# Sketch attention and a cosine router: queries sketched like keys, token rows scattered to expert regions, ten expert blocks placed among the attention's ticks

## The chip, the cores and the metric

The kernel runs on one core of a Trainium2 chip. The metric is the device time of one execution in microseconds (us); less is better. The engines are PE (TensorE: matmul; PEld is its weight load), DVE (VectorE), ACT (ScalarE), POOL (GpSimd) and SP (SyncE, which issues DMAs). Each works through its own queue in order.

## The reference

Polynomial sketch attention is followed by a router that sends each token to one of eight experts. All data is f32.

```python
# q, k, v: (4, 4, 1088, 32); S1, S2: (8, 32); expert_emb: (8, 128); w1: (8, 128, 1024); w2: (8, 1024, 128)
def phi(x):
    a = einsum('rd,bhsd->bhsr', S1, x); b = einsum('rd,bhsd->bhsr', S2, x)
    return einsum('bhsi,bhsj->bhsij', a, b).reshape(..., 64)
q_p, k_p = phi(q), phi(k)
kv = einsum('bhsf,bhsd->bhfd', k_p, v);  z = sum(k_p, axis=2)
attn = einsum('bhsf,bhfd->bhsd', q_p, kv) / (einsum('bhsf,bhf->bhs', q_p, z)[..., None] + 1e-6)
x = attn.transpose(0, 2, 1, 3).reshape(4352, 128)
xn = x / (norm(x) + 1e-6);  en = expert_emb / (norm(expert_emb) + 1e-6)
logits = xn @ en.T / tau
idx = argmax(logits, 1);  probs = softmax(logits)
out[idx == e] = probs[:, e] * (relu(x[idx == e] @ w1[e]) @ w2[e])    # for each expert e
```

## The kernel before

The four batches are taken as two pairs (`NM = 2`, index m). A token of a pair is one of 128 partitions in one of 17 chunks (`NC`), so a pair has 17 chunks of 128 tokens and the whole 34 (`NT`). Chunks are worked on in groups of three or four (`K_GROUPS`, `Q_GROUPS`; the last key group has one).

**Loads.** SP issues all loads in order: keys and values of pair 0, its queries, the same for pair 1, then the weights of the eight experts. Keys and queries land one head at a time in `k_sb` and `q_sb`, where the four heads of a chunk lie side by side.

**Keys** (`k_steps`): `tr` turns each chunk with a transpose, `ab` makes both sketches of a chunk in one product with `Sblk` (L270), ACT copies the second sketch to `b_sb`, DVE multiplies the two into the 64 features per head, `kp` (L276), and `kv` sums `kp` times v and a column of ones into PSUM (L288). `kz` is the masked sum of a pair.

**Queries** (`q_steps`): `tr` turns a chunk; `fa` and `fb` (L328) make the features already transposed and as wide as they are after the outer product, with `Sa` and `Sb`, up to 512 tokens at once; their product is `qp` (L340); `nd` multiplies it with `kz` on column halves of the array (L348) and divides, which gives the token rows `x`; `xt` turns those, ACT sums their squares (`ssq`, L367), and `logit` gives eight logits per token (L372).

**Routing.** `pick(m)` finds the expert of each token of a pair as a one-hot `oh`; `gate_tokens(m)` divides by the norm (a square root as a power of one half on POOL, L399), takes the softmax value, multiplies it into the token rows on POOL (L408) and stores them to `x_dram` through SP (L410). After both pairs, `route_and_run_experts` counts and ranks all tokens per expert (L418 to L449), builds the list of tokens of each of 41 blocks (`NBLK`) of 128 slots by one-hot products (L462 to L490), and has `src_i` (rows to fetch), `dst_i` (rows to write) and `exp_i` (the expert of a block). An expert's tokens fill whole blocks; unused slots write nowhere.

**Expert blocks.** Block i: `fetch` gathers 128 rows of `x_dram` with an indirect DMA from POOL (L497), four blocks ahead (`AHEAD`); `turn` transposes them (L503); `weights` copies the expert's weights within SBUF on DVE (L512, L513); `up` has eight products and a Relu on ACT (L522, L523); `down` has eight products (L529), a copy to `y` (L531) and an indirect DMA that scatters the rows to `out` (L532). On PE the order is up(i), turn(i+1), down(i-1).

**Order.** In attention, `put` enters each step in a table of ticks, but a scheduler may move instructions; only from `route_and_run_experts` on are DVE and PE kept in the order written. ACT and POOL are ordered by the scheduler throughout.

Of the kernel before, what the change touches and what calls it, by code (L numbers as in the profile page):

```python
# [21 lines left out]
R = 8  # L22
# [11 lines left out]
K_GROUPS = ((0, 4), (4, 8), (8, 12), (12, 16), (16, 17))  # L34
Q_GROUPS = ((0, 4), (4, 8), (8, 11), (11, 14), (14, 17))
# [3 lines left out]
NOWHERE = 8192.0  # L39
DIGIT = 128  # L40
# [9 lines left out]
def kernel(  # L50
# [28 lines left out]
    def ps_acc(i):  # L79
        return psum.tile([P, 512], F32, tag=f"acc{i}", bufs=1, name=f"ps_acc{i}")  # L80
# [6 lines left out]
    def rows_tile(name):  # L87
        return rows_p.tile([P, NC, H, D], F32, tag="rows", name=name)

    def load_q(m):  # L90

        for i in range(2):
            for h in range(H):
                nc.sync.dma_start(
                    q_sb[m][i * HALF:(i + 1) * HALF, :, h],
                    bass.AP(tensor=q.tensor, offset=q.offset + ((2 * m + i) * H + h) * S * D,
                            ap=[[NC * D, HALF], [D, NC], [1, D]]))


    v_sb = [consts.tile([P, 6, NC, D], F32, name=f"v{m}") for m in range(NM)]  # L100

    def load_k(m, i):
        for h in range(H):
            nc.sync.dma_start(
                k_sb[m][:, i * NK:(i + 1) * NK, h],
                bass.AP(tensor=k.tensor, offset=k.offset + ((2 * m + i) * H + h) * S * D,
                        ap=[[NK * D, P], [D, NK], [1, D]]))

    def load_v(m, i):
        for p in range(2):  # L110
            nc.sync.dma_start(
                v_sb[m][:, 3 * p:3 * p + 2, i * NK:(i + 1) * NK],
                bass.AP(tensor=v.tensor, offset=v.offset + ((2 * m + i) * H + 2 * p) * S * D,
                        ap=[[NK * D, P], [S * D, 2], [1, NK * D]]))

    def load_rest(m):
        for i in range(2):
            r = slice(i * HALF, (i + 1) * HALF)
            at = (2 * m + i) * H * S * D + SK * D
            nc.sync.dma_start(k_sb[m][r, NC - 1],  # L120
                              bass.AP(tensor=k.tensor, offset=k.offset + at, ap=[[D, HALF], [S * D, H], [1, D]]))
            for p in range(2):
                nc.sync.dma_start(v_sb[m][r, 3 * p:3 * p + 2, NC - 1],
                                  bass.AP(tensor=v.tensor, offset=v.offset + at + 2 * p * S * D,
                                          ap=[[D, HALF], [S * D, 2], [1, D]]))
# [4 lines left out]
    for m in range(NM):  # L130
        k_sb[m] = rows_tile(f"k{m}")
        for i in range(2):
            load_k(m, i)
            load_v(m, i)
        load_rest(m)
        q_sb[m] = rows_tile(f"q{m}")
        load_q(m)
        if m == 0:
            nc.sync.dma_start(emb_sb[:], emb)
            nc.sync.dma_start(tau_sb[:], bass.AP(tensor=tau.tensor, offset=tau.offset, ap=[[0, E], [1, 1]]))  # L140
# [9 lines left out]
    for m in range(NM):  # L150
        for p in range(2):
            nc.gpsimd.memset(v_sb[m][:, 3 * p + 2], 1.0)

    mask4 = consts.tile([P, H], F32, name="mask4")
    maskh = consts.tile([P, 2], F32, name="maskh")
    for t in (mask4, maskh):
        nc.vector.memset(t, 0.0)
    for h in range(H):
        nc.vector.memset(mask4[h * D:(h + 1) * D, h:h + 1], 1.0)
    for h in range(2):  # L160
        nc.vector.memset(maskh[HALF * h:HALF * (h + 1), h:h + 1], 1.0)
# [28 lines left out]
    nc.vector.tensor_copy(ST, ps[:, :2 * R])  # L190

    Sblk = consts.tile([P, 6, 2 * R], F32, name="Sblk")
    nc.vector.memset(Sblk, 0.0)
    nc.vector.tensor_mul(Sblk[:, :H], bview(ST, [[0, H], [1, 2 * R]]), bview(mask4, [[1, H], [0, 2 * R]]))
    Sa = consts.tile([P, H, R, R], F32, name="Sa")
    Sb = consts.tile([P, H, R, R], F32, name="Sb")
    for h in range(H):
        nc.vector.tensor_scalar_mul(Sa[:, h], bview(ST, [[1, R], [0, R]]), mask4[:, h:h + 1])
        nc.vector.tensor_scalar_mul(Sb[:, h], bview(ST[:, R:], [[0, R], [1, R]]), mask4[:, h:h + 1])

    half_c = consts.tile([P, NC], F32, name="half_c")
    nc.gpsimd.memset(half_c, 0.5)
    x_dram = tc.dram_tile([N, DM], F32, name="x_dram")

    def iota(shape, pattern, base, mult, name):
# [6 lines left out]
    lane = iota([P, P], [[1, P]], 0, 0, "lane")  # L212
    part = iota([P, 1], [[1, 1]], 0, 1, "part")
    first = iota([P, E], [[-1, E]], E, 0, "first")
    start = iota([P, NT], [[P, NT]], 0, 0, "start")
    lane_b = consts.tile([P, P], BF16, name="lane_b")
    nc.vector.tensor_copy(lane_b, lane)
    tok_i = consts.tile([P, 3, NT], I32, name="tok_i")
    nc.gpsimd.iota(tok_i[:, 0].rearrange("p (m c) -> p m c", m=NM), pattern=[[2 * S, NM], [1, NC]], base=1,
                   channel_multiplier=NC)  # L220
    nc.vector.tensor_scalar(tok_i[:, 1], tok_i[:, 0], 7, None, op0=ALU.logical_shift_right)
    nc.vector.tensor_scalar(tok_i[:, 2], tok_i[:, 0], DIGIT - 1, None, op0=ALU.bitwise_and)
    tok_d = consts.tile([P, 2, NT], F32, name="tok_d")
    nc.vector.tensor_copy(tok_d, tok_i[:, 1:])
    digits = [tok_d[:, d] for d in range(2)]
    before = consts.tile([P, P], F32, name="before")
    nc.vector.tensor_scalar(before, lane, part[:, 0:1], None, op0=ALU.is_gt)
    ones = consts.tile([P, P], F32, name="ones")
    nc.vector.memset(ones, 1.0)
    follows = consts.tile([P, E, NT], F32, name="follows")  # L230
    nc.vector.memset(follows, 1.0)
    nc.vector.memset(follows[:, :, 0:1], 0.0)

    enT = consts.tile([P, 96], F32, name="enT")
    nc.vector.memset(enT, 0.0)

    def prep_emb():
# [4 lines left out]
        nc.gpsimd.tensor_tensor(out=ss, in0=ss, in1=half_c[:E, 0:1], op=ALU.pow)  # L242
# [7 lines left out]
        nc.vector.tensor_copy(enT[:, :E], ps[:, :E])  # L250


    kz = {}
    acc = {}

    def k_steps(m, c0, c1):
# [3 lines left out]
        def tr():  # L260
            ps = ps_small()
            for j in range(n):
                nc.tensor.transpose(ps[:, j * P:(j + 1) * P], k_sb[m][:, c0 + j].rearrange("p h d -> p (h d)"), ident)
            s["kT"] = work.tile([P, 512], F32, tag="xT", name="kT")
            nc.scalar.copy(s["kT"][:, :n * P], ps[:, :n * P])

        def ab():
            ps = ps_small().rearrange("p (j g r) -> p j g r", j=4, r=2 * R)
            for j in range(n):
                nc.tensor.matmul(ps[:, j, :6], s["kT"][:, j * P:(j + 1) * P], Sblk, start=True, stop=True)  # L270
            b_sb = work.tile([P, 4, H, R], F32, tag="b", name="b_sb")
            nc.scalar.copy(b_sb[:, :n], ps[:, :n, :H, R:])  # L272
            s["kp"] = work.tile([P, 4, H, R, R], F32, tag="kp", name="kp")
            for j in range(n):
                a, b = ps[:, j, :H, :R], b_sb[:, j]
                nc.vector.tensor_mul(s["kp"][:, j],  # L276
                                     bview(a, [list(a.ap[1]), list(a.ap[2]), [0, R]]),
                                     bview(b, [list(b.ap[1]), [0, R], list(b.ap[2])]))

        def kv():  # L280
            if c0 == 0:
                acc[m] = [ps_acc(i)[:, :6 * D].rearrange("p (a n) -> p a n", a=2) for i in range(2)]
            for c in range(c0, c1):
                rest = c == NC - 1
                for i in range(2) if rest else (c // NK,):
                    r = slice(i * HALF, (i + 1) * HALF) if rest else slice(0, P)
                    for p in range(2):
                        nc.tensor.matmul(  # L288
                            acc[m][i][:, p],
                            s["kp"][r, c - c0, 2 * p:2 * p + 2].rearrange("s h i j -> s (h i j)"),  # L290
                            v_sb[m][r, 3 * p:3 * p + 3, c],
                            start=c == i * NK and p == 0, stop=rest, skip_group_check=True)
            if c1 == NC:
                for i in range(2):

                    z = consts.tile([P, 2, 2, D + 1], F32, name=f"kz{2 * m + i}")
                    t = acc[m][i]
                    nc.vector.tensor_mul(z[:, :, :, :D], t[:, :, :2 * D].rearrange("p a (h d) -> p a h d", h=2),
                                         bview(maskh, [[0, 2], [1, 2], [0, D]]))
                    zs = t[:, :, 2 * D:2 * D + 1]  # L300
                    nc.vector.tensor_mul(z[:, :, :, D], bview(zs, [list(zs.ap[1]), [0, 2]]),
                                         bview(maskh, [[0, 2], [1, 2]]))
                    kz[2 * m + i] = z.rearrange("p a h d -> p a (h d)")
        return [tr, ab, kv]

    x_sb = {}
# [266 lines left out]
    for i in sorted(at):  # L573
        for f in at[i]:
            f()
# [33 lines left out]
```

## Time and profile before

| | |
|---|---|
| median of 3 runs (lowest, highest) | 307.86 us (307.71, 309.45) |
| profiled execution | 309.62 us, span 307.8 us, granted TensorE clock 0.916 |
| busy in the span | PE 254.5, PEld 230.3, DVE 140.1, POOL 107.2, ACT 86.5 us |
| L522 and L529 (expert products) | 656 records each, 83.6 and 79.8 us |
| L497, L532 (indirect DMAs on POOL) | 41 each, mean 1.17 and 1.01 us |
| L523, L531 (ACT in a block) | mean 1.03 and 0.27 us |
| L512, L513 (weight copies on DVE) | 41 each, mean 0.69 us |
| L340 (qp, 1024 wide), L276 (kp, 256 wide) on DVE | mean 1.21 and 0.42 us |
| loads | 17.8 MB read from HBM; queue q1 24.2% of 16 engines' time |

A row of a group has its line, engine and operation, the tiles by name (out<-in), the shape and count, then busy time, mean duration of one in ns, and the engine's idle time just ahead of them with what ended it. A row of the timeline has its start, its duration, and in brackets the idle time ahead. A window has its length, the busy time and count of each engine, the granted clock, and the share and rate of the DMA engines. A product in f32 shows as two matmul records, a transpose as one. Durations of records on PE overlap.

### The profile page before, as it was taken

What the parts mean: (1) busy time and instruction counts of PE and PEld (TensorE: products, weight loads), DVE (VectorE), ACT (ScalarE), POOL (GpSimd) and SP (SyncE); (2) the same over time, 40 slices, a digit from 0 to 9 for tenths busy, and PEclk for the clock granted to TensorE, in tenths of its full rate; (3) what the DMA queues carried; (4) which work ended last, traced back from release to release, by engine and by line L of the source; (5) the groups of instructions that cost most, each with busy time, mean ns of one, the idle gap of its engine ahead of it and who ended that gap; (6) DMA issues with size and microseconds to landing.
All of it is one profiled execution on the core that took longest, in us unless ns stands there. A gap on an engine that the chain in (4) does not pass through costs nothing. (4 is left out here: it accounts for less than half of the span.)

```text
span 307.8 us, 5515 instructions
## 1 busy us (share of the span) xinstructions
PE 254.5 (83%) x2127; PEld 230.3 (75%) x2127; DVE 140.1 (46%) x345; ACT 86.5 (28%) x195; POOL 107.2 (35%) x103
## 2 busy tenths in 40 slices
PE   0987999999799750125999999999999999999960
PEld 0886777776467530114999999999999999999960
DVE  7334254345464448982344444444444444444400
ACT  1121242332245210001133333333333333333320
POOL 4000000000413034017455666555666556632230
PEclk9999799999999955555799999999999999999995
DMA  6999799993003001102111111111111111210000
GB/s 122 167 136 171 146 135 327 336 345 85 0 2 145 1 2 66 79 0 48 30 34 38 34 37 28 36 30 44 37 30 37 34 40 32 36 25 19 15 2 0
DMA packets 51194, 22.59 MB, mean 73 GB/s; under 512 B 38425, under 2 KB 48676, under 8 KB 50912
## 3 DMA queue, kind: packets, MB, share of 16 engines
q1 hardware_dynamic: 48544, 17.31, 24.2%
q0 software_dynamic: 2624, 4.92, 6.2%
q8 instruction: 17, 0.28, 0.4%
q14 instruction: 9, 0.07, 0.1%
HBM read 17.77 MB, written 4.92 MB: 74 GB/s over the span
## 5 line engine op out<-in xcount | busy, mean ns | idle before, releaser
L522 PE MATMUL ps_big<-xTb,w1b 128*128 128x128 f32 x656 | 83.6, 283 | 1.7 <-issue 1.3
L522 PEld LDWEIGHTS ps_big<-xTb,w1b 128*128 128x128 f32 x656 | 79.8, 199 | 2.4 <-issue 1.7
L529 PE MATMUL ps_acc<-w2b,hT 128*128 128x128 f32 x656 | 79.8, 275 | 0.0
L529 PEld LDWEIGHTS ps_acc<-w2b,hT 128*128 128x128 f32 x656 | 76.4, 192 | 0.0
L523 ACT ACTIVATE hT<-ps_big 128x1024 f32<-128x1024 f32 x41 | 42.1, 1027 | 94.6 <-PE ps_big L522 83.6
L497 POOL DMA_INDIRECT xs<-x_dram,src_i x41 | 48.0, 1170 | 39.4 <-PE ps_t L503 21.4
L532 POOL DMA_INDIRECT out_dram<-y,dst_i x41 | 41.4, 1010 | 50.3 <-ACT y L531 48.4
L505 DVE COPY xTb<-ps_t 128x128 f32<-128x128 f32 x41 | 12.0, 292 | 75.0 <-PE ps_t L503 75.0
L512 DVE COPY w1b<-w_sb 128x1024 f32 x41 | 28.5, 694 | 13.5 <-DVE xTb L505 12.1
L399 POOL TENSOR_TENSOR nrm<-ssq,half_c 128x17 f32<-128x17 f32 x2 | 6.2, 3087 | 65.7 <-ACT sq L367 65.7
L513 DVE COPY w2b<-w_sb 128x1024 f32 x41 | 28.5, 694 | 0.0
L340 DVE TENSOR_TENSOR qp<-a_sb,ps_big 128x768 f32<-128x768 f32 (+1 forms) x10 | 10.6, 1055 | 23.4 <-PE ps_big L328 20.3
L531 ACT COPY y<-ps_acc 128x128 f32<-128x128 f32 x41 | 11.0, 267 | 33.9 <-PE ps_acc L529 33.9
L288 PE MATMUL ps_acc<-v,kp 128*128 128x96 f32 (+1 forms) x144 | 19.8, 295 | 0.8 <-DVE kp L276 0.8
L288 PEld LDWEIGHTS ps_acc<-v,kp 128*128 128x128 f32 (+1 forms) x144 | 18.2, 206 | 2.9 <-DVE kp L276 1.6
L276 DVE TENSOR_TENSOR kp<-ps_t,b_sb 128x256 f32<-128x256 f32 x34 | 12.1, 418 | 14.5 <-ACT b_sb L272 14.5
L469 PE MATMUL ps_acc<-col,row 128*128 128x82 bf16 x34 | 3.0, 269 | 18.3 <-DVE row L466 18.3
L328 PE MATMUL ps_big<-qT,Sa 128*128 128x384 f32 (+1 forms) x40 | 17.3, 556 | 0.0
L367 ACT ACTIVATE sq<-x 128x128 f32<-128x128 f32 x34 | 10.3, 308 | 24.2 <-DVE x L356 24.2
L469 PEld LDWEIGHTS <-row 128*128 128x128 bf16 x34 | 2.3, 138 | 19.7 <-DVE row L466 19.7
L328 PE MATMUL ps_big<-qT,Sb 128*128 128x384 f32 (+1 forms) x40 | 16.5, 534 | 0.0
L503 PE MATMUL ps_t<-ident,xs 128*128 128x128 f32 x41 | 11.5, 281 | 4.2 <-DMA xs<-x_dram,src_i 4.2
(137 smaller groups left out, 220.3 us busy)
## 6 DMA issues: line engine op xcount, KB each, us to landing
w_sb<-in_moe_w_dram SPq DMA_DIRECT2D x16, 512.0 KB, 8.3
q<-in_q_dram SPq DMA_DIRECT2D x16, 136.0 KB, 4.2
x_dram<-x SPq DMA_DIRECT2D x2, 1088.0 KB
k<-in_k_dram SPq DMA_DIRECT2D x16, 128.0 KB, 3.8
v<-in_v_dram SPq DMA_DIRECT2D x8, 256.0 KB, 3.3
xs<-x_dram,src_i POOLq DMA_INDIRECT x41
out_dram<-y,dst_i POOLq DMA_INDIRECT x41
k<-in_k_dram SPq DMA_DIRECT2D x4, 32.0 KB, 3.4
```

What stands on the lines that cost most here:

```text
L276: nc.vector.tensor_mul(s["kp"][:, j], bview(a, [list(a.ap[1]), list(a.ap[2]), [0, R]]), bview(b, [list(b.ap[1]), [0, R], list(b.ap[2])]))
L288: nc.tensor.matmul(acc[m][i][:, p], s["kp"][r, c - c0, 2 * p:2 * p + 2].rearrange("s h i j -> s (h i j)"), v_sb[m][r, 3 * p:3 * p + 3, c], ...
L328: nc.tensor.matmul(ps[:, p, :w], S_[:, 2 * p:2 * p + 2].rearrange("p h i j -> p (h i j)"), s["qT"][:, :w], start=True, stop=True)
L497: nc.gpsimd.indirect_dma_start(out=xs[i][:], out_offset=None, in_=x_dram[:, :], in_offset=bass.IndirectOffsetOnAxis(ap=src_i[:, i:i + 1], ...
L503: nc.tensor.transpose(ps[:, :P], xs.pop(i), ident)
L505: nc.vector.tensor_copy(xT[i], ps[:, :P])
L512: nc.vector.tensor_copy(w1b[i], w1_sb[:, bass.ds(e, 1)].rearrange("p o f -> p (o f)"))
L513: nc.vector.tensor_copy(w2b[i], w2_sb[:, bass.ds(e, 1)].rearrange("p o f d -> p (o f) d"))
L522: nc.tensor.matmul(ps[:, u, j * P:(j + 1) * P], w[:, f * P:(f + 1) * P], x, start=True, stop=True)
L523: nc.scalar.activation(hT[i], ps, ACT.Relu)
L529: nc.tensor.matmul(ps, h[:, f * P:(f + 1) * P], w[:, f], start=f == 0, stop=f == NF - 1)
L532: nc.gpsimd.indirect_dma_start(out=out[:, :], out_offset=bass.IndirectOffsetOnAxis(ap=dst_i[:, i:i + 1], axis=0), in_=y[:], in_offset=None ...
```

## The change

- **Loads and keys.** `k_sb`, `q_sb` hold each head's chunks side by side, so one transpose turns four chunks of one head, and one DMA loads a batch's keys. The seventeenth chunk has tiles of its own (`k_rest`, `q_rest`). v has one column of ones per pair.
- **Queries like keys.** `Sa` and `Sb` are gone. Queries go through the same `turned`, `sketch`, `second`, `features` as keys; a new step `tr_qp` transposes the features, two per chunk.
- **Column halves.** `sketch`, `kv` and `logit` have 64-column stationary operands whose outputs lie in one or the other half of the PSUM partitions.
- **Rows in regions.** The token rows with their eight logits, the sum of squares and the token's number are 138 words in `xg`. `router` picks experts for eight chunks at a time, ranks them with running counts, and `place` scatters each chunk (one indirect DMA on POOL per 128 rows) into the region of its expert in `rows`. `table_early` and `table_late` compute only which region rows a block has.
- **Early blocks.** Ten blocks (`EARLY`) need only full blocks of pair 0's tokens; `table_early` names them, and the others come from `table_late`.
- **Gate at y.** A block computes norm, Exp and sum for its own rows (`norm` with a power on POOL, `up`, `share`), and the gate is the scale of the copy to `y`. The output row's number is the last word of the fetched row.
- **Order.** All of attention, routing and blocks are entered in one table, and PE, DVE, ACT and POOL are kept in that order.

```diff
-K_GROUPS = ((0, 4), (4, 8), (8, 12), (12, 16), (16, 17))
-Q_GROUPS = ((0, 4), (4, 8), (8, 11), (11, 14), (14, 17))
+GROUPS = ((0, 4), (4, 8), (8, 12), (12, 16), (16, 17))
+SPAN = 8
+ROW = DM + E + 2
+EARLY = (NM * NC * P // 2 - E * (P - 1) + P - 1) // P
+LATE = NBLK - EARLY
...
+    def sketch(ps, t, n):
+        for u in range(2):
+            r = slice(u * HALF, (u + 1) * HALF)
...
+                for h in range(H):
+                    nc.tensor.matmul(ps[r].rearrange("p (g h r) -> p g h r", h=H, r=2 * R)[:, :, h],
+                                     t[:, h * P + u * HALF:h * P + (u + 1) * HALF], Sblk, start=True, stop=True)
...
+    def features(ab, b, n, tag):
+        t = work.tile([P, 4, H, R * R], F32, tag=tag, name=tag)
+        nc.vector.tensor_mul(t[:, :n].rearrange("p j h (i k) -> p (j h) i k", i=R),
+                             ab[:, :, 0].unsqueeze(3).broadcast_to([P, n * H, R, R]),
+                             b[:, :n * H].unsqueeze(2).broadcast_to([P, n * H, R, R]))
...
+    def keys(m, c0, c1, put, late):
...
+        put(0, 60, tr)
+        put(1, 51, ab)
+        put(1, 61, b)
+        put(1, 63, prod)
+        put(5 if late else 3, 30, kv)
...
+    def queries(m, c0, c1, put):
...
         def tr():
+            if at == 0:
+                xg[g] = work.tile([P, SPAN, ROW], F32, tag="xg", bufs=3, name="xg")
+            s["qT"] = turned(None if n == 1 else q_sb[m][:, :, c0:c0 + 4], q_rest[m], n, "qT")
+            nc.gpsimd.iota(xg[g].bitcast(I32)[:, own, ROW - 1], pattern=[[1, n]], base=2 * S * m + c0,
+                           channel_multiplier=NC)
...
+        put(0, 61, tr)
+        put(1, 50, ab)
+        put(1, 60, b)
+        put(1, 62, prod)
+        put(3, 10, tr_qp)
+        put(4, 20, nd)
+        put(5, 20, xt)
+        put(5, 80, squares)
+        put(6, 10, logit)
+        put(6, 70, best)
+        if c1 == NC or c1 % SPAN == 0:
+            pick, place = router(m, c1 - at - n, c1)
+            put(6, 71, pick)
+            put(7, 40, place)
...
+        def place():
...
             for j in range(n):
+                d = nc.gpsimd.indirect_dma_start(
+                    out=rows[:, :], out_offset=bass.IndirectOffsetOnAxis(ap=slot[:, j:j + 1], axis=0),
+                    in_=xg[m, c0 // SPAN].bitcast(I32)[:, j], in_offset=None)
+                tc.add_to_no_dep_group("rows", d.ins)
+                if m > 0:
+                    tc.add_to_no_dep_group("early", d.ins)
...
+    def norm(i):
+        rn[i] = work.tile([P, 1], F32, tag="rn", bufs=3, name="rn")
+        nc.gpsimd.tensor_tensor(out=rn[i], in0=xs[i][:, DM + E:DM + E + 1], in1=half_c, op=ALU.pow)
+        nc.vector.tensor_scalar_add(rn[i], rn[i], NORM_EPS)
+        nc.vector.reciprocal(rn[i], rn[i])
...
+    def up(i):
...
         nc.scalar.activation(hT[i], ps, ACT.Relu)
+        p = work.tile([P, E], F32, tag="probs", name="probs")
+        gate[i] = work.tile([P, 1], F32, tag="gate", bufs=3, name="gate")
+        nc.scalar.activation(p, xs[i][:, DM:DM + E], ACT.Exp, scale=rn.pop(i)[:, 0:1], accum_out=gate[i])
...
+    def share(i):
+        nc.vector.tensor_scalar_add(gate[i], gate[i], PROB_EPS)
+        nc.vector.reciprocal(gate[i], gate[i])
...
+    def first_block():
         for i in range(AHEAD):
             fetch(i)
+        norm(0)
         weights(0)
         turn(0)
...
+    def block(i):
+        if i + AHEAD < NBLK:
+            fetch(i + AHEAD)
+        if i < NBLK:
+            up(i)
+        if i + 1 < NBLK:
+            turn(i + 1)
+            weights(i + 1)
+        if i < NBLK:
+            share(i)
+        if i + 1 < NBLK:
+            norm(i + 1)
+        if i > 0:
+            down(i - 1)
...
     tick = 0
+    for g in GROUPS:
+        keys(0, *g, put_at(tick), True)
         tick += 2
+    put_at(tick)(0, 0, prep_emb)
+    for g in GROUPS:
+        keys(1, *g, put_at(tick), False)
+        queries(0, *g, put_at(tick))
         tick += 2
+    put_at(tick)(5, 90, table_early)
+    put_at(tick)(8, 90, first_block)
+    for g in GROUPS:
+        queries(1, *g, put_at(tick))
+        tick += 2
+    put_at(tick)(5, 50, table_late)
+    for i in range(NBLK + 1):
+        put_at(tick)(i - 1, 55, lambda i=i: block(i))
```

The first number of `put` is the tick after the group's own, the second the rank within the tick. So keys of pair 0 start at ticks 0 to 8, keys of pair 1 and queries of pair 0 at 10 to 18, queries of pair 1 at 20 to 28; scatters stand in ticks 19, 23, 25 (pair 0) and 29, 33, 35 (pair 1), eight, eight and one; block i stands in tick 29 + i. The sketches of a tick's keys and queries share one PSUM bank, "ab".

## The prediction

> **What bounds the kernel now.** I read the page's slices first, then busy time by stretches, then the groups by shape, and last the timeline around the routing and at the start of the expert blocks.
>
> ```profile
> PE   0987999999799750125999999999999999999960
> PEclk9999799999999955555799999999999999999995
> 100.00:110.00 10.00, 7.60 (x77) 5.62 (x75) 3.87 (x11) 3.53 (x15) 0.80 (x1) 0.96 0.00 1
> 110.00:120.00 10.00, 2.28 (x5) 1.18 (x4) 7.51 (x20) 0.32 (x1) 4.90 (x2) 0.50 0.01 2
> 120.00:130.00 10.00, 0.79 (x9) 0.61 (x9) 9.52 (x20) 0.00 (x0) 1.21 (x1) 0.50 0.27 111
> 130.00:140.00 10.00, 2.25 (x25) 1.69 (x25) 7.92 (x18) 0.00 (x0) 2.31 (x2) 0.50 0.02 7
> 160.00:170.00 10.00, 10.00 (x92) 10.00 (x91) 3.95 (x8) 3.62 (x5) 6.20 (x6) 1.00 0.13 36
> ```
>
> The columns of a stretch are its length, the busy time of PE, PEld, DVE, ACT and POOL with instruction counts, the granted clock, the DMA share and GB/s. The span has four stages: attention to 110.2 us (PE nearly full), routing to 141.4 (a chain on DVE; PE idle, clock 0.50), 41 expert blocks to 297.6 (PE full; a block starts every 3.68 us: its second halves start at 150.26, 153.94, 157.63), and 10.2 us from PE's last product to the end.
>
> ```profile
> L270 PE MATMUL ps_t<-Sblk,kT 128*128 128x96 f32 x68 | 13.1, 335 | 1.4 <-ACT kT L265 1.4
> L399 POOL TENSOR_TENSOR nrm<-ssq,half_c 128x17 f32<-128x17 f32 x2 | 6.2, 3087 | 65.7 <-ACT sq L367 65.7
> L340 DVE TENSOR_TENSOR qp<-a_sb,ps_big 128x1024 f32<-128x1024 f32 x4 | 4.8, 1206 | 9.5 <-PE ps_big L328 9.5
> L242 POOL TENSOR_TENSOR emb_ss<-emb_ss,half_c 8x1 f32<-8x1 f32 x1 | 0.6, 575 | 18.3 <-ACT emb_sq L241 18.3
> ```
> ```profile
> 75.88 1.98 PE L328 MATMUL ps_big<-qT,Sa 128*128 128x512 f32 x4
> 88.37 1.03 PE L372 MATMUL ps_t<-enT,xT 128*128 128x96 f32 x8
> 89.59 1.21 PE L348 MATMUL ps_big<-kz,qp 128*64 128x66 f32 x32 [0.19 <-DVE qp L340]
> 117.37 3.84 POOL L408 TENSOR_TENSOR x<-x,gate 128x2176 f32<-128x2176 f32 x1 [5.10 <-DVE gate L407]
> 118.04 3.20 DVE L434 TENSOR_TENSOR_SCAN upto<-ones,nb 128x8 f32<-128x8 f32 x1
> 143.15 0.95 POOL L497 DMA_INDIRECT xs<-x_dram,src_i  x1 [0.30 <-issue]
> 144.40 0.95 POOL L497 DMA_INDIRECT xs<-x_dram,src_i  x1 [0.30 <-issue]
> 152.90 1.02 POOL L532 DMA_INDIRECT out_dram<-y,dst_i  x1 [1.02 <-ACT y L531]
> 154.49 1.19 POOL L497 DMA_INDIRECT xs<-x_dram,src_i  x1 [0.57 <-PE ps_t L503]
> ```
>
> Mean durations overlap, so I take pitches from runs of one group: (1.21-0.22)/31 = 0.03 us for a product on a column half, (1.03-0.28)/7 = 0.11 for a full 128-column one, (1.98-0.64)/3 = 0.43 to 0.45 for 512 wide. Each f32 product is two records, a transpose one. POOL issues an indirect DMA every 1.25 us (0.95 + 0.30).
>
> **PE.** Per four chunks the keys cost 28 x 0.11 = 3.1 us before; now 4 transposes, 16 records in ab and 32 in kv on halves: 0.44 + 48 x 0.03 = 1.9. Queries: 16 x 0.11 + 32 x 0.03 + 8 x 0.43 = 6.2 before; now Sa and Sb go, 8 transposes of qp come, ab and logit go to halves: 16 x 0.11 + 64 x 0.03 = 3.7. Over 8.5 groups that is 9.3 against 5.6, 31 us less PE work. If eight neighbours on one half don't overlap (ab only), 16 x 0.03 more, 8 us in all, mostly off the path. Logits at 0.03 is the nearest row; at 0.06, 4 us.
>
> The Trainium skill (TensorEngine Tiling (Array Packing), Key Properties) says that changing the tiling mode drains the array, which speaks against mixing halves and full products. Here the step from the last L348 record to the next full product was 0.15 us (83.913 to 84.063) against 0.03 inside the group; two switches per pair of ticks make 2 us over attention, and I keep them out of the sum, since PE doesn't set the pace there.
>
> **Routing.** L382 to L490, 31.2 us of idle PE, goes; so do the two x_dram stores on SP and both 3.8 us multiplies on POOL. In their place: per eight chunks a pick (some 1.3 us of DVE) and a place (0.7 us), two tables on DVE (13 ops, 3 us; 22 ops, 5.6 us, by rows of 0.17 to 0.48), and 34 scatters on POOL at 1.25 = 42 us. Ten blocks need only batches 0 and 1. SP issues 12 loads per pair of batches instead of 26, in longer pieces; by the 330 GB/s of 50 to 70 us the data of each stage lands ahead of it (at 150 GB/s, the early rate, the last keys land near 40, still in time).
>
> **When the first scatter starts.** Keys begin at 5.9. The one "ab" bank is held from ab through prod, so a group costs 0.5 + 0.25 + kb 0.27 + 0.1 + 1.2 (L340) = 2.4; five with a cold start end near 18.5. prep_emb stands ahead of tick 10's transposes: ACT, POOL, DVE in turn, 2.3 more. A pair of ticks with keys and queries cycles through ab 0.5, 0.25, qb 0.27, both products 2.4, nd on DVE 1.1, xt 0.43, kv 1.0, with hand-overs 6.15 us; PE needs 5.6, ACT 5.5, DVE 5. Pairs of 2.9, 5.0, 6.15, 6.15 bring tick 18 to 41, and nd, best, pick and place of tick 19 take 6.3: 47.3. Bounds: 38 by PE work alone, 58 at the old 9.3 per pair.
>
> **POOL's queue to the first block.** It is now in order by hand. Eight scatters, 10.0; the iota of tick 20 rewrites the same buffer (three xg, six used), so it waits for them to land, 1.5 + 0.5 (L497 from 137.39 landed at 140.5, 1.6 after its end); eight more, 10.0; the iota of tick 24, 2.2; the one scatter of tick 25, 1.25; the iota of tick 28, 2.0; four fetches, 5.0; pow and hand-over, 0.9. That is 33.4. DVE's norm(0) stands ahead of weights(0) and turn(0), 0.35 + 0.3 + 1.4 + 0.3: the first up starts at 83. PE and ACT alone would be there at 72 (Q1 pairs of 5 us, by ACT's 4.64: 2.0 of it squares). Bounds: a scatter at 1.0 or 1.5 gives 78 or 88.
>
> **First up to the eighth, tick 29 to 36.** Their PE work is 7 x 3.68 + 4 of queries = 30 us. But tick 29's eight scatters stand ahead of fetch(4) and pow(1): DVE waits in norm(1) until +13, behind it nd, behind that PE's xt. From there POOL goes fetch, pow, scatter per block; tick 33 puts eight more scatters ahead of pow(5) (near +38), norm(6) near +41, then pick and place; table_late's 5.6 us end near +49, and weights(7) lets up(7) go at +51. Bounds 30 (all hidden) and 65 (scatters at 1.5, pow at its high end of a few per block).
>
> **The other 34 blocks.** PE 3.68 each. POOL per block: fetch 1.2, pow, scatter 1.02, gaps of 0.30. L242 (one element in 8 lanes) gives pow 0.58, L399 (17 in 128) 3.09; two rows make 0.42 + 0.16 per element, so 0.58 is nearest: 3.4 us, hidden by 0.28. pow may also meet DVE's weight copies, as L434 met L408 above (3.2 us for eight numbers): up to 0.7 more, 0.4 per block uncovered, 14 us. ACT (1.03 + 0.5 + 0.27) and DVE (0.29 + 1.4 + 0.6) stay under 3.68. So 34 x 3.68 + 1.95 = 127. The last scatter loses its wait for the one before (297.97 to 299.29): the tail goes from 10.2 to 9.1. After idle spells the clock was 0.50 (110 to 150 us); 1 us for that, 0 to 5.
>
> **Sum.** 83 + 51 + 127 + 9 + 1 = 271 us of span, against 307.8. The profiled execution took 309.6, 1.8 more than its span, and the median of the runs is 1.8 below it, so the forecast of the median is 271.
>
> The rows show an indirect DMA of 1.19 us beside the weight copies (154.49) and of 0.95 without (143.15): 0.25, already in the sum. The Trainium skill (SBUF — State Buffer, Summary: rules for kernel authors) holds that GpSimd's descriptor writing starves while DVE runs a fast copy, which speaks against the change. With the 3.1 us that SBUF — State Buffer (A bandwidth-pool intuition that's wrong) gives for such an overlap, an estimate for the 34 scatters would pass 330 us. I go by the rows.
>
> **Rivals.** *POOL hides:* scatters and waits for xg stay behind other work. For it: POOL is idle until tick 19. Against: the iota and norm chains above. Then 72 + 30 + 127 + 9 = 238.
>
> *Half-way:* pow meets the copies and the last 34 blocks take up to 4.1: 271 + 14 = 285, and up to 300 with scatters at 1.5 (+5 and +7).
>
> *Slower:* POOL sets the pace of every block. Place: fetch, pow, scatter in one queue. At pow 3.09, 5.9 per block: 83 + 3 + 51 + 17 + 34 x 5.9 + 11 = 366. It loses to before from pow = 1.65 on (34 x 0.8 + 8 x 1.07 = 36); or from 0.37 more per indirect DMA (52 x 0.37 early, 34 x 0.52 late), which rows of 552 instead of 512 bytes could bring. For it: L399; against: L242, and 1.0 on every L532.
>
> *The change doesn't do what it says:* early fetches wait for the late scatters. They stand ahead of them in POOL's queue, so they can't.
>
> **How the numbers follow.** Forecast (262 to 282) 0.50; hidden 0.17; half-way 0.20; slower 0.13. 243 leaves about 0.1 of "hidden" below, 300 about 0.1 above. Faster by over 1% 0.85, within 1% 0.02, slower 0.13; the runs before spread by 0.6%, so about 1% can be told.
>
> **What would show it.** Right: POOL's scatters in rows of eight 1.25 apart, the first near 47; DVE waiting on POOL's pow for 10 us twice; PE with a hole near 75 to 83 and thin slices to 134; blocks 3.68 apart after that. Wrong: blocks wider than 3.7 (POOL per block), up(0) before 75 (hidden), or scatters above 1.5.

## The result, and the profile after

The changed kernel takes 333.51 us (median of 4 runs, 332.59 to 334.52) against 307.88 us before: ratio 1.0825, 95% interval 1.0777 to 1.0873. It is slower by 8%; the forecast was 271 us, faster. The profiled execution has a span of 330.7 us.

The slices of the changed kernel (page, part 2) come first: PE, POOL and the granted clock.

```profile
PE   2967887803910391049650099999999999999992
POOL 4010001332332523373433638888888888888632
PEclk9999999965585678558795569999999999999998
```

Before, PE had one hole of 31 us. Now it has four: slices of 8.3 us with 0 or 1 between 65 and 190 us, with the granted clock at 0.5 or 0.6 of full speed somewhere in each. From 196 us on PE is full, as before. Four stretches by engine (columns as in the stretches before):

```profile
70.00:80.00 10.00, 0.00 (x0) 0.00 (x0) 0.73 (x2) 0.00 (x0) 3.11 (x6) 0.50 0.06 21
100.00:110.00 10.00, 0.00 (x0) 0.00 (x0) 2.18 (x8) 0.00 (x0) 4.21 (x7) 0.50 0.08 24
130.00:140.00 10.00, 0.00 (x0) 0.00 (x0) 0.00 (x0) 0.00 (x0) 3.36 (x4) 0.53 0.06 21
250.00:300.00 50.00, 49.99 (x449) 49.83 (x448) 28.71 (x93) 23.05 (x55) 42.64 (x42) 1.00 0.14 36
```

In the holes POOL works about a third of the time (3.1 to 4.2 of 10 us), DVE less (0 to 2.2), the others not at all: this is a chain of waits, not a lack of engine time. POOL's timeline shows what it does in the holes, and the fetches after it:

```profile
55.09 1.07 POOL L475 DMA_INDIRECT rows_dram<-xg,slot  x1 [33.15 <-ACT sq L402]
58.27 0.97 POOL L475 DMA_INDIRECT rows_dram<-xg,slot  x1 [2.11 <-ACT xT L397]
61.33 0.96 POOL L475 DMA_INDIRECT rows_dram<-xg,slot  x1 [2.09 <-DMA rows_dram<-xg,slot]
64.38 0.96 POOL L475 DMA_INDIRECT rows_dram<-xg,slot  x1 [2.10 <-ACT lg L413]
...
109.13 0.96 POOL L563 DMA_INDIRECT xs<-rows_dram,src  x1 [0.30 <-issue]
110.40 0.95 POOL L563 DMA_INDIRECT xs<-rows_dram,src  x1 [0.30 <-issue]
```

A scatter (L475) takes the same 0.96 us of POOL as a fetch (L563), but 2.1 us of idle time stand ahead of it instead of 0.30. The pitch is 3.06 us (about 2.6 in the last row of eight), where the forecast had 1.25. The second and fourth row name ACT as the releaser; ACT had long been done with that span's rows, and the 2.1 us are the same whoever is named. It is the landing of the scatter before. The waits (in all, times, longest) and the groups carry the bill:

```profile
DVE rn L587 <- POOL rn L586: 56.0, 33, 21.9
POOL rows_dram L475 <- DMA rows_dram<-xg,slot: 43.0, 22, 2.2
DVE xg L389 <- DMA rows_dram<-xg,slot: 25.4, 2, 13.8
```
```profile
L586 POOL TENSOR_TENSOR rn<-xs,half_c 128x1 f32<-128x1 f32 x41 | 33.4, 815 | 0.9
...
L475 POOL DMA_INDIRECT rows_dram<-xg,slot x34 | 33.3, 980 | 98.6 <-DMA rows_dram<-xg,slot 43.0 <-ACT sq L402 33.1 <-DVE slot L473 6.9
```

DVE stands up to 21.9 us in `norm`, because the power stands in POOL's queue behind a row of eight scatters. Here are the last of them, a fetch and the power on POOL, then DVE:

```profile
139.52 0.96 POOL L475 DMA_INDIRECT rows_dram<-xg,slot  x1 [2.14 <-DMA rows_dram<-xg,slot]
142.29 0.98 POOL L563 DMA_INDIRECT xs<-rows_dram,src  x1 [1.80 <-DMA rows_dram<-xg,slot]
143.29 0.57 POOL L586 TENSOR_TENSOR rn<-xs,half_c 128x1 f32<-128x1 f32 x1
143.90 0.15 DVE L587 TENSOR_SCALAR rn<-rn 128x1 f32<-128x1 f32 x1 [21.92 <-POOL rn L586]
```

Also `nd` (L389) waits 13.8 us for scatters that still read the `xg` buffer that it is to write. Behind DVE stands PE.

By stage, in us of the profiled execution (first scatter, 17th scatter, first products of up(0) and up(7), PE's last product, end of the span):

| kernel | scatter 1 | scatter 17 | up(0) | up(7) | PE end | end | median of runs |
|---|---|---|---|---|---|---|---|
| forecast | 47.3 | | 83 | 134 | 261 | 271 | 271 |
| the change | 55.1 | 104.7 | 116.3 | 196.9 | 324.3 | 330.7 | 333.5 |
| rows_declared | 54.7 | 84.8 | 100.4 | 158.2 | 285.6 | 292.2 | 297.0 |
| all_declared | 57.3 | 87.4 | 103.0 | 160.8 | 288.2 | 292.3 | 294.1 |
| two_per_tick | 57.4 | 87.1 | 103.0 | 152.3 | 284.5 | 288.5 | 289.5 |
| norms_and_two_per_tick | 58.6 | 88.9 | 101.7 | 144.9 | 274.5 | 278.6 | 278.5 |

Ratios and their intervals compare fast runs with fast runs, while a median is over all runs of a kernel: of the four of `norms_and_two_per_tick`, two were slow (280.46, which is the one profiled, and 281.0 us), and the fast ones took 273.86 and 276.45.

### The profile page after: what moved, and what is told of

The parts are those of the page before. It is cut to its first block, busy times and chain, and to the rows that moved or that the text cites. A ratio compares the mean times of both kernels' runs of the same rounds, so it can differ in the third digit from the quotient of the medians.

```text
span 330.7 us, 6634 instructions
## 1 busy us (share of the span) xinstructions
PE 231.2 (70%) x2507; PEld 220.9 (67%) x2507; DVE 143.9 (44%) x492; ACT 108.8 (33%) x305; POOL 161.9 (49%) x186
## 4 chain that ended last, share of the span: by engine, by line
POOL 24%; issue 22%; PE 20%; DMA 20%; DVE 10%; ACT 2%; POOLq 1%; DVEq 0%; SPq 0%
DMA rows_dram<-xg,slot 14%; POOL xs L563 11%; POOL rn L586 9%; PE ps_ab L277 4%; DMA out_dram<-y,xs 4%; POOL out_dram L616 4%; PE ps_big L597 3%; PE ps_acc L324 3%; PE ps_t L264 2%; DVE qp L288 2%; PE ps_t L395 2%; PE ps_big L381 2%; DVE kp L288 1%; DVE xg L389 1%; DMA k<-in_k_dram 1%
## 5 line engine op out<-in xcount | busy, mean ns | idle before, releaser
L475 POOL DMA_INDIRECT rows_dram<-xg,slot x34 | 33.3, 980 | 98.6 <-DMA rows_dram<-xg,slot 43.0
L563 POOL DMA_INDIRECT xs<-rows_dram,src x41 | 46.5, 1133 | 20.5 <-issue 11.7
L616 POOL DMA_INDIRECT out_dram<-y,xs x41 | 43.2, 1053 | 25.1 <-issue 9.1
L612 PE MATMUL ps_ab<-w2b,hT 128*128 128x128 f32 x320 | 41.0, 284 | 0.0
L612 PE MATMUL ps_acc<-w2b,hT 128*128 128x128 f32 x336 | 41.0, 275 | 0.0
L612 PEld LDWEIGHTS ps_ab<-w2b,hT 128*128 128x128 f32 x320 | 39.6, 202 | 0.0
L612 PEld LDWEIGHTS ps_acc<-w2b,hT 128*128 128x128 f32 x336 | 39.2, 192 | 0.0
L586 POOL TENSOR_TENSOR rn<-xs,half_c 128x1 f32<-128x1 f32 x41 | 33.4, 815 | 0.9
L370 PE MATMUL ps_big<-ident,qp 128*128 128x128 f32 x68 | 11.3, 315 | 20.3 <-ACT probs L602 19.2
L602 ACT ACTIVATE probs<-xs,rn 128x8 f32<-128x8 f32 x41 | 12.0, 292 | 33.6 <-DVE rn L588 33.6
```

What stands on the lines that cost most here:

```text
L370: nc.tensor.transpose(ps[:, p, j * P:(j + 1) * P], s["qp"][:, j, 2 * p:2 * p + 2].rearrange("p h f -> p (h f)"), ident)
L475: d = nc.gpsimd.indirect_dma_start(out=rows[:, :], out_offset=bass.IndirectOffsetOnAxis(ap=slot[:, j:j + 1], axis=0), in_=xg[m, c0 // SPAN ...
L563: d = nc.gpsimd.indirect_dma_start(out=xs[i].bitcast(I32)[:], out_offset=None, in_=rows[:, :], in_offset=bass.IndirectOffsetOnAxis(ap=src[ ...
L586: nc.gpsimd.tensor_tensor(out=rn[i], in0=xs[i][:, DM + E:DM + E + 1], in1=half_c, op=ALU.pow)
L612: nc.tensor.matmul(ps, h[:, f * P:(f + 1) * P], w[:, f], start=f == 0, stop=f == NF - 1)
L616: d = nc.gpsimd.indirect_dma_start(out=out[:, :], out_offset=bass.IndirectOffsetOnAxis(ap=x.bitcast(I32)[:, ROW - 1:], axis=0), in_=y[:], ...
```

## The experiments

Theory: each scatter waits for the one before it to land, and the change says otherwise but doesn't bring it about. `tc.add_to_no_dep_group` only gives an instruction a group's name; the wait is lifted by `tc.declare_no_dep`, which the change never calls. The waits above name the DMA of a scatter as what POOL's next scatter waited for. First rival: it is the power of each block, in POOL's queue, that holds DVE.

**The control, and the cause.** In both runs a tiny memset on POOL stands ahead of each scatter. `spacers_only` has the memset alone, `rows_declared` the declaration as well, so that the declaration is the only difference between the two.

```diff
 for j in range(n):
+    nc.gpsimd.memset(spacer, 0.0)           # both; spacer is 128x1
     d = nc.gpsimd.indirect_dma_start(out=rows[:, :], ...)
+    tc.declare_no_dep(d.ins, group="rows", reason="other rows")   # rows_declared only
     tc.add_to_no_dep_group("rows", d.ins)
```

> The changed kernel with one small memset on POOL ahead of each of the 34 scatters and nothing else; a control for the next two runs, which need it. Theory A (each scatter stands in POOL's queue until the scatter before it has landed, because naming a group lifts no wait): the memsets run while the queue waits, so 331 to 337 us, scatters still about 3.06 us apart. Theory B (POOL's own work per block, fetch, power and scatter, sets the pace): 34 x 0.1 more, 334 to 338.

> The same with each scatter declared independent of the earlier ones. Theory A: scatters 1.3 us apart; first scatter near 55 as before; up(0) near 93 instead of 116; up(7) some 51 us after that instead of 80; the last 34 blocks 127 us as now; 272 to 285 us. Theory B: POOL does the same work, so 325 us or more. If attention's slower pairs (7.1 us instead of 6.15) were the cause, the gain would be under 10 us.

Measured: 335.49 us with the memsets alone (one run, before 308.81 beside it; the first eight scatters are 3.12 us apart), and 296.99 us with the declaration (293.99 to 298.34; 0.9641 of before, interval 0.9574 to 0.9708). POOL's timeline in `rows_declared`:

```profile
54.71 1.07 POOL L476 DMA_INDIRECT rows_dram<-xg,slot  x1 [33.04 <-ACT sq L402]
55.78 0.11 POOL L475 MEMSET spacer<- 128x1 f32 x1
56.08 0.96 POOL L476 DMA_INDIRECT rows_dram<-xg,slot  x1 [0.19 <-issue]
57.04 0.11 POOL L475 MEMSET spacer<- 128x1 f32 x1
57.35 0.96 POOL L476 DMA_INDIRECT rows_dram<-xg,slot  x1 [0.19 <-issue]
```

The pitch is 1.27 us. The declaration is worth 38.5 us (36.5 against the changed kernel). Against the changed kernel up(0) comes 15.9 us earlier, the way from up(0) to up(7) is 22.8 us shorter, and the rest is unchanged. But the time missed what was expected of it by 12 us or more; that is followed up below.

**The other two groups.** `all_declared` does the same for the early fetches against the scatters of pair 1 and for the scatters to `out`.

```diff
+    tc.declare_no_dep(d.ins, group="early", reason="other rows")   # fetches of early blocks, scatters of pair 1
+    tc.declare_no_dep(d.ins, group="out", reason="other rows")     # scatters to out
```

> As before, and the early fetches are declared independent of pair 1's scatters and the other way round, and the output scatters of each other. Theory A: fetch(4) and fetch(8) need not wait for eight scatters to land (about 2 us each), the tail loses its two waits of 1.9 us: 4 to 8 us below the run with rows alone. Theory B: no difference beyond 2 us.

Measured: 294.05 us (0.9524, 0.944 to 0.9608), some 3 us less, where 4 to 8 were expected and the intervals overlap. The landing waits ahead of two early fetches (1.59 and 2.07 us in `rows_declared`) are gone, and the way from PE's end to the end of the span is 4.1 us instead of 6.7; the last two output scatters no longer wait 2.1 and 1.9 us for the one before.

**The rival: the power.** `no_power` is the changed kernel with a copy on DVE where the power was; it leaves the square root out.

```diff
-    nc.gpsimd.tensor_tensor(out=rn[i], in0=xs[i][:, DM + E:DM + E + 1], in1=half_c, op=ALU.pow)
+    nc.vector.tensor_copy(rn[i], xs[i][:, DM + E:DM + E + 1])
```

> The changed kernel with the power of one half left out of each block's norm (a copy on DVE stands there, so the gate is another). Theory A: POOL's waits for landings stay, 325 to 334 us. Theory B: 41 x 0.82 = 33 us less POOL work, near 300 us.

Measured: 318.25 us (one run), between the two ranges. The first up is at 116.8 us, not earlier; with the first scatter 2.3 us later, the way between them is 1.8 us shorter, so the power has little part in the first chain. The gain lies between up(0) and up(7), 51.4 us instead of 80.5, since DVE no longer stands behind POOL; 14.5 of it are given back later (141.9 us instead of 127.4 for the last 34 blocks), when fetches come late from POOL's queue. Seven powers of 0.6 us would be 4 of those 29 us: the power adds to the loss mainly through its place behind the scatters.

**What still stood above the forecast.** In `rows_declared`, with scatters of 1.27 us, PE's timeline shows something that neither theory had:

```profile
59.00 0.34 PE L410 MATMUL ps_t<-enT,xT 128*64 128x8 f32 x4 [0.39 <-issue]
60.47 0.31 PE L410 MATMUL ps_t<-enT,xT 128*64 128x8 f32 x4 [1.12 <-issue]
61.91 0.28 PE L410 MATMUL ps_t<-enT,xT 128*64 128x8 f32 x2 [1.14 <-issue]
...
63.34 0.27 PE L381 MATMUL ps_big<-kz,qpT 128*64 128x66 f32 x1 [0.91 <-issue]
64.08 0.27 PE L381 MATMUL ps_big<-kz,qpT 128*64 128x66 f32 x1 [0.47 <-issue]
```

These products wait for nothing, yet they come in small lots 0.7 or 1.4 us apart, from the fourth scatter of the row until the last one has landed. Summed over PE's timeline from 50 to 170 us, idle stretches of over 0.3 us that nothing but "issue" ends make 11.2 us in `rows_declared`, 12.5 in `all_declared`, and 0 in the changed kernel and in `spacers_only`. Of the 11.2, 0.9 lie outside the rows of eight, behind four fetches at the same pitch. Four kernels tell the reasons apart.

**Norms with the rows, two scatters per tick, both, and a wider row.** `norms_with_rows` takes the power for four chunks at once in the query ticks and lets 1/(norm + eps) travel in the row. `two_per_tick` spreads a row of eight over four ticks and has five `xg` buffers. Both start from `all_declared`; `rows_spaced` starts from `rows_declared`.

```diff
+        def norms():                                              # norms_with_rows, put(6, 20, norms)
+            nrm = xg[g][:, own, DM + E]
+            nc.gpsimd.tensor_tensor(out=nrm, in0=nrm, in1=half_c.broadcast_to([P, n]), op=ALU.pow)
+            nc.vector.tensor_scalar_add(nrm, nrm, NORM_EPS)
+            nc.vector.reciprocal(nrm, nrm)
...
     def norm(i):
+        rn[i] = xs[i][:, DM + E:DM + E + 1]
```
```diff
-        xg[g] = work.tile([P, SPAN, ROW], F32, tag="xg", bufs=3, name="xg")    # two_per_tick
+        xg[g] = work.tile([P, SPAN, ROW], F32, tag="xg", bufs=5, name="xg")
...
+            for j in range(0, at + n, 2):
+                put(7 + j // 2, 41, lambda j=j: scatter(j))
```
```diff
-    spacer = consts.tile([P, 1], F32, name="spacer")             # rows_spaced
+    spacer = consts.tile([P, 1024], F32, name="spacer")
```

> Base: the kernel all_declared (294.1 us), every scatter and fetch independent. The power is taken for four chunks at once (128x4) in the query ticks, ahead of the scatters, and the finished 1/(norm+eps) travels in the row; the power, the add and the reciprocal go out of the expert blocks. Theory A (what is left above the forecast is DVE standing in norm(i+1) behind a power that POOL's queue holds behind eight scatters: waits of 7.5 and 6.9 us in all_declared): the steps up(1) to up(2) and up(6) to up(7), 12.2 and 12.6 us there, fall to under 8, up(7) comes 10 to 20 us earlier, 275 us (268 to 285). Theory B (it is the rows of eight scatters themselves, which hold back the fetches, and PE's slow feed beside them): within 5 us of 294. Either way POOL's work per block falls from 3.68 to about 2.8, and the last 34 blocks stay at 3.68 each.

> Base: all_declared. The eight scatters of a span go out two per tick over four ticks instead of eight in a row, and xg has five buffers instead of three, so no iota waits for a landing. Theory B (rows of scatters 1.27 us apart slow PE's feed to one f32 product per 0.72 us, 12.5 us of PE's idle time put down to issue between 50 and 170 us, and hold the fetches back): that sum falls below 4 us, the first up starts near 92 instead of 103, and the time is 280 us (272 to 288). Theory A (the power's place decides): the first up moves by less than 5 us and the time stays within 6 us of 294.

> Both edits. If A and B are separate causes their gains add: 262 us (254 to 272), up(7) near 125 and 34 blocks at 3.68 behind it. If they are one and the same wait, no better than the better one of the two by over 4 us.

> Base: the kernel rows_declared (297.0 us), where each scatter is independent of the one before. The spacer between two scatters is a memset of 128x1024 instead of 128x1, about 1.05 us by 0.56 for 128x544, so that the scatters of a row go out 2.2 us apart and still wait for nothing. If the density of the scatters slows PE's feed: PE's idle time put down to issue between 50 and 170 us, 11.2 us in rows_declared, falls below 4. If any scatter that waits for nothing does it, each one costs as much as before and the sum stays near 11. Time: the rows of eight take 7.6 us more each, four of them partly on the path, less what PE gets back: 300 to 318.

Measured, against before in the same set (310.49 us): `norms_with_rows` 297.83 us (0.9626, 0.951 to 0.9742), `two_per_tick` 289.47 (0.9341, 0.925 to 0.9431), both together 278.45 (0.8889, 0.8766 to 0.9013), `rows_spaced` 312.78 (one run).

`rows_spaced` bears on PE's feed. Its scatters still wait for no landing:

```profile
59.91 0.97 POOL L476 DMA_INDIRECT rows_dram<-xg,slot  x1 [0.17 <-ACT qpT L373]
60.87 0.98 POOL L475 MEMSET spacer<- 128x1024 f32 x1
62.01 0.97 POOL L476 DMA_INDIRECT rows_dram<-xg,slot  x1 [0.17 <-ACT sq L402]
```

At a pitch of 2.10 us PE's idle time put down to issue is 0 instead of 11.2 us. So it takes scatters as dense as those; that they are untied is not enough. The same sum is 6.7 in `two_per_tick`, 4.0 with both edits, and 2.3 in `norms_with_rows`, whose first two rows are as dense, but PE mostly has nothing to do there (11.6 us of waiting for DVE in the first). It is 0 in `late_blocks_untied` and `whole_columns` below, whose rows are broken in the same way as with both edits. So how long a dense row must be, and what else must meet it, was not measured. What in the chip it is that slow PE's feed (a DMA queue, memory, POOL itself) is left open.

`norms_with_rows` alone brought nothing (the interval overlaps that of `all_declared`; theory A expected it to save 9 to 26 us, and theory B's "within 5 us of 294" holds). The two steps that theory A would have under 8 us are 11.81 and 13.85, little changed (the second is from up(5) to up(6), not to up(7) as the expectation has it). The waits show why: the power for four chunks still stands behind a row of eight scatters, only in another place. POOL's timeline, then DVE's:

```profile
66.83 0.96 POOL L483 DMA_INDIRECT rows_dram<-xg,slot  x1 [0.19 <-DMA rows_dram<-xg,slot]
67.81 1.06 POOL L407 TENSOR_TENSOR xg<-xg,half_c 128x4 f32<-128x4 f32 x1
```
```profile
68.90 0.17 DVE L408 TENSOR_SCALAR xg<-xg 128x4 f32<-128x4 f32 x1 [11.16 <-POOL xg L407]
```

DVE waits 11.16 us for a power of 1.06. Theory A had the right victim and the wrong cure: not the power's length or count matters, but eight scatters ahead of it. With the rows broken up the same edit is worth 11 us in the medians (289.47 to 278.45) and 14 by the ratios, more than the 9 us that A named as the least. `two_per_tick` alone gave 4.6 us instead of the 14 that theory B expected. Its up(0) did not move (103.0), as theory A had it, but that doesn't decide: the edit did not bring about what it was for, and PE's feed still cost 6.7 us. POOL's timeline there:

```profile
61.26 0.96 POOL L482 DMA_INDIRECT rows_dram<-xg,slot  x1 [0.19 <-issue]
62.23 0.15 POOL L354 IOTA xg<- 128x4 int32 x1
62.58 0.98 POOL L482 DMA_INDIRECT rows_dram<-xg,slot  x1 [0.16 <-issue]
```

Ticks are an order, not times. Between the scatters of two ticks POOL's queue had only an iota that waited for nothing, so the eight still left in a row. The powers of `norms_with_rows`, which wait for ACT, break that row: from the first scatter to the eighth it is 13.5 us instead of 9.0, and 4.0 us of PE's feed are lost instead of 6.7. So the two edits need each other; still, 262 us (254 to 272) was expected, and even the fastest run took 273.86.

**Is the early start worth it?** `late_blocks` is the changed kernel, `late_blocks_untied` is `norms_and_two_per_tick`, both with all 41 blocks behind the last scatter.

```diff
-    put_at(tick)(8, 90, first_block)        # after the ticks of pair 0
     for g in GROUPS:
         queries(1, *g, put_at(tick))
...
+    put_at(tick)(6, 90, first_block)        # after the ticks of pair 1
     for i in range(NBLK + 1):
-        put_at(tick)(i - 1, 55, lambda i=i: block(i))
+        put_at(tick)(i + 7, 55, lambda i=i: block(i))
```

> Base: the changed kernel (333.5 us) as it is, chained scatters and all. The ten early blocks are not started early: the first fetch stands behind the last scatter and the last table, as all 41 blocks do. Theory A (with scatters 3.06 us apart POOL's chain of 34 sets the time of the last scatter, and the early blocks only fill PE while it goes on): 17 scatters end near 105 as now, 17 more end near 165, the first up starts near 176, and 41 blocks of 3.68, 2 and the tail of 6.4 end near 335 (325 to 342): the early start is worth nothing here. Theory B (the early blocks' fetches, powers and output scatters delay the later scatters in POOL's queue, so that the early start costs time): 322 or less. Theory C (the early start is worth the PE time of its seven blocks): 355 or more.

> The same edit on norms_and_two_per_tick (278.5 us). By its trace the last scatter ended at 151 with seven blocks among the ticks; without them near 120, the first up near 128, and 41 blocks of 3.68 with 8 to the end make 287 (280 to 296): the early start is worth some 9 us. If PE has so little to do in the attention of batches 2 and 3 that the early blocks are worth their full 7 x 3.68 = 26 us: 300 or more. If they only delay the rest: 275 or less.

Measured: 336.83 us (1.0852, 1.0732 to 1.0973) against 1.0825 with the early start, and 283.85 us (0.9184, 0.9099 to 0.9269) against 0.8889. POOL's timeline of `late_blocks`, where the last scatter ends and the first fetch follows:

```profile
159.50 0.96 POOL L475 DMA_INDIRECT rows_dram<-xg,slot  x1 [2.09 <-DMA rows_dram<-xg,slot]
162.57 0.96 POOL L475 DMA_INDIRECT rows_dram<-xg,slot  x1 [2.11 <-DMA rows_dram<-xg,slot]
165.22 1.00 POOL L563 DMA_INDIRECT xs<-rows_dram,src  x1 [1.70 <-DMA rows_dram<-xg,slot]
```

The chain of 34 scatters ends at 163.5 us and the first up is at 173.3, as expected within 3 us; from the third block on the blocks are 3.7 us apart. In the changed kernel ten blocks among the ticks gain nothing that can be measured, since they push the last scatter from 162.6 to 190.9. Untied, they gain 9 us by the ratios, as expected, and 5 in the medians.

**Column halves.** `whole_columns` has the two sketches on all 128 columns again, on top of `norms_and_two_per_tick`.

```diff
-        for u in range(2):
-            r = slice(u * HALF, (u + 1) * HALF)
...
-                    nc.tensor.matmul(ps[r].rearrange(...)[:, :, h],
-                                     t[:, h * P + u * HALF:h * P + (u + 1) * HALF], Sblk, start=True, stop=True)
+                    nc.tensor.matmul(ps.rearrange(...)[:, :, h],
+                                     t[:, h * P:(h + 1) * P], Sblk, start=True, stop=True)
```

> Base: norms_and_two_per_tick (278.5 us). The products of ab on column halves go back to products over all 128 columns: half as many, 16 records of L277 for a group instead of 32 where keys and queries meet. In the changed kernel 32 of these on halves took 1.3 us, since eight neighbours share a half, against the 0.5 of the forecast; whole ones at 0.11 make 0.9. Theory A (ab is a link of the ring ab, features, nd, xt, kv that sets the 7.1 us pair of ticks): pairs 0.4 us shorter, the first scatter about 1.5 us earlier, 276 (272 to 278). Theory B (halves are worth what the forecast gave them): pairs longer by 0.4, 280 or more.

Measured: 279.41 us (0.9014, 0.8915 to 0.9114), no difference that can be told from 0.8889 (0.8766 to 0.9013), as the intervals overlap. Where keys and queries meet and the clock is full, the 32 records on halves take 1.49 us (`norms_and_two_per_tick`) and the 16 whole ones 2.00. So halves are the cheaper form by 0.5 us per pair, against my theory A, whose 0.9 took a record's pitch for a product's; and it isn't seen in the end. In this run the granted clock was 0.50 from 30 to 40 us, among the early pairs, which put the first scatter at 67.8 us instead of 58.6, and yet up(7) is only 2.2 us later.

## Why the prediction was wrong

**The step that failed** is "a scatter at 1.25 us" in "POOL's queue to the first block", used again in "First up to the eighth", with bounds of 1.0 and 1.5. It was read from fetches, which depend on nothing among themselves, while scatters write one tensor. A scatter that waits for the one before it has a price in the trace of before: the last output scatter's wait, which I named with 297.97 to 299.29, and the L497 that landed 1.6 us after its end. I took the change's no-dependency group at its word. That price is in these two lines of before; the start-to-start step is 2.88 us, 1.90 of it idle:

```profile
296.41 0.98 POOL L532 DMA_INDIRECT out_dram<-y,dst_i  x1 [2.59 <-ACT y L531]
299.29 0.98 POOL L532 DMA_INDIRECT out_dram<-y,dst_i  x1 [1.90 <-DMA out_dram<-y,dst_i]
```

In its place the runs showed a pitch of 3.06 us, because each scatter waited for the landing of the one before; declared independent, the scatters go out 1.27 us apart and the kernel takes 297.0 us. Of the 62.5 us above the forecast this gives back 36.5; the other 26 are among the terms below.

- *First scatter:* 47.3 forecast, 55.1 measured, inside its bounds of 38 and 58. Pairs of ticks take 7.13 us instead of 6.15 (ab starts at 31.62, 38.76, 45.89). The mis-sized term is ab: 1.49 us for its 32 records, not 0.5, which is 16 records at 0.03; ACT's copy of the queries' sketch starts only after all 32. The two pairs before these, forecast at 2.9 and 5.0, took 6.92 and 7.14 from ab to ab (the first at 24.70); why the first of them is that long was not separated.
- *POOL's queue, first scatter to the first power's end:* 33.4 forecast, 58.1 measured, 39.2 with untied scatters. What remains of the excess is a wait of 5.6 us for the second span's slots, which come after PE's slow feed; how much of the wait the feed makes was not separated.
- *up(0):* 83 forecast (78 to 88), 116.3 measured, 100.4 untied. Of the 17.4 left, 7.4 is the first scatter, 5.8 POOL's queue, and 4.2 the way from the power to up.
- *up(0) to up(7):* 51 forecast (30 to 65), 80.5 measured, 57.7 untied. The mechanism was as described, DVE held in `norm` by a power behind eight scatters; its size followed the pitch.
- *The last 34 blocks with PE's end:* 127 forecast, 127.4 measured, and in `late_blocks` 127.3. POOL's part of a block is in the timeline of the changed kernel:

```profile
221.26 1.22 POOL L563 DMA_INDIRECT xs<-rows_dram,src  x1 [0.30 <-issue]
222.50 0.89 POOL L586 TENSOR_TENSOR rn<-xs,half_c 128x1 f32<-128x1 f32 x1
223.60 1.03 POOL L616 DMA_INDIRECT out_dram<-y,xs  x1 [0.21 <-issue]
```

- *The power:* 0.58 was right where DVE is quiet (0.57 to 0.61), and 0.89 in the median beside the weight copies, inside the 0.7 more allowed for that. With it POOL has no wait over 0.30 us in a block of 3.68, but PE still sets the pace, since taking the power out of the blocks (`norms_with_rows`) left them at 3.68.
- *The tail:* 9.1 forecast, 6.5 measured. The forecast that the last scatter loses its wait was wrong in the changed kernel (1.90 us ahead of it) and right in `all_declared`. The tail is shorter for another reason, which stays open: from the last scatter's end to the end of the span it is 2.4 us, and was 7.6 before.

**The rivals.** "POOL hides" and "Half-way" did not come: up(0) is at 116.3 us, not 72, and the last 34 blocks keep 3.68 us each. "Slower" lost its place: POOL doesn't set the pace of the blocks. But its condition, "0.37 more per indirect DMA", was met by a factor of five in the 34 scatters, for a reason that it didn't name. "The change doesn't do what it says" was asked only of fetches against scatters and answered by their order in the queue; that order doesn't excuse a scatter from waiting for a scatter. This rival, asked of all three groups, would have been the right one: at 3.06 instead of 1.25 a row of eight is 14.5 us longer, and two rows stand ahead of up(0) and two more ahead of up(7).

The Trainium skill (DMA: Bandwidth & Descriptors, Anatomy of one DMA — SWDGE (gpsimd) path) gives a DMA a fixed cost of about 2.0 us, most of it the time until the write is confirmed, and says that a wait for it is served on the issuing engine's sequencer. The 2.1 us of idle time ahead of most L475 (1.6 in the last row) are of that size. The rule that I weighed in the prediction, on descriptor writing beside DVE's fast copies (SBUF — State Buffer, Summary: rules for kernel authors), shows here as a fetch of 1.22 instead of 0.95 us, far from 3.1. That the estimate made from it, over 330 us, lies near the 333.5 measured is luck: a scatter took 0.96 us on POOL, and the 3.06 us steps stand also where DVE does nothing at all (130 to 140 us).

**What stays open.** The best version found, `norms_and_two_per_tick`, takes 278.45 us, 11% less than before by the ratio and 7 more than the forecast. In the profiled execution it reaches up(7) at 144.9 instead of 134. Its remaining waits between scatter 1 and up(0) are spread over POOL, ACT and a granted clock of 0.66 to 0.68 from 60 to 100 us, and were not separated.

## What to carry to other kernels

A DMA that follows another one on the same queue costs its issue; one that waits for it costs the landing as well, here 3.06 us against 1.27. So before a row of DMAs is priced, find out whether each is really free of the one before, from a row of the same kind that writes one tensor in a profile; a name for a group is not a declaration. In a queue kept by hand, the price of a short instruction is what stands ahead of it: a power of 0.6 us held DVE for 21.9.

## What the runs showed that I had not expected

- Untied scatters 1.27 us apart slow PE's feed to lots of products 0.7 or 1.4 us apart: 11.2 us of PE's idle time, nearly all in the rows, and 0 at a pitch of 2.10 or 3.06. Faster DMA issue was partly paid for by the engine that it was to serve.
- Seven blocks' worth of PE work done early, 26 us, gained nothing in the changed kernel (1.0825 against 1.0852 without), since each block put its DMAs and power into the queue that sets the end.
- A power on POOL takes 0.57 to 0.61 us for one element per lane and 1.06 for four (`norms_with_rows`), under half as much per element; beside DVE's weight copies the one-element form takes 0.89 in the median.
